# Two attentions on one core: an earlier place for ScalarE's copy in double steps, and B's output products in single steps

## The chip, the cores and the metric

The kernel runs on one core of one Trainium2 chip. The metric is the device time of one execution in microseconds. Before the change it was 1608.44 us, the median of 3 runs (1606.99 to 1608.65). The phase that the change touches runs from about 420 us to 1600 us of the profiled execution.

## What is computed

Two independent attention blocks over 2048 positions of width 576, with 32 heads of 18 columns each, side by side in the output:

```python
def _A_ref(x, wqkv, wo):            # window of 8 positions, 2 apart
    qkv = (x @ wqkv).reshape(B, S, 3, H, Dh)...
    logits = einsum("bhsd,bhswd->bhsw", q, kg) * scale      # kg, vg: 8 gathered positions
    attn = softmax(where(mask, logits, -1e9))
    return einsum("bhsw,bhswd->bhsd", attn, vg)... @ wo

def _B_ref(x, wqkv, wo):            # every position sees every position
    p = softmax(einsum("bhqd,bhkd->bhqk", q, k) * scale)
    return einsum("bhqk,bhkd->bhqd", p, v)... @ wo

return concatenate([a, b], axis=-1)
```

All inputs are fp32. The kernel splits fp32 operands of its matmuls into a rounded upper part and a remainder, and makes each product as three matmuls (upper by upper, upper by rest, rest by upper).

## The kernel before

**Three phases.** First the projections of both attentions (TensorE, until about 420 us). Then 512 steps in which B is computed and A runs beside it, mostly on GpSimd. Then a short close.

**A step.** B's work is ordered by head group (8 groups of 4 heads, `g`), block of 512 queries (4 blocks, `b`) and tile of 128 keys (16 tiles, `kt`). For one step TensorE makes four score matmuls, one per head (L269, into a bank of the ring "scores"), ScalarE makes four exponentials of them (L277, into tiles `e`), and TensorE makes the weighted sums of the step before it (`weigh`, L742): four matmuls side by side, one per head, on 32 columns each, into one bank `po` that collects the 16 steps of a block. A score works on 56 of 64 rows of the array; two of them, on the upper and the lower 64 rows, run side by side.

**The maxima.** The exponentials need a bound of each query's scores ahead of time. For that the scores of later blocks are computed a second time, in pieces (L158), and VectorE reduces each piece (L166, one bank at a time). A step takes three pieces: one behind the first score, one split over two halves (`parts_of_maximum`), and one behind the last score. In TensorE's program these stand among the scores. When all pieces are done (`sum(given) == total`), the steps are "paired": the weighted sums of two steps follow each other.

**The banks.** Seven PSUM banks in two rings: four for "scores", three for "else" (pieces, products). The eighth is `po`. An instruction of TensorE that takes a bank waits until ScalarE or VectorE has read what was there.

**Output products.** A product of 128 positions by 288 output columns with `wo` takes two strands of some 14 (A) or 15 (B) matmuls, one on the upper and one on the lower 64 rows. There are three ways in which they stand in the order:
- In a *double step* (`together`, L1174 to 1214): two steps are written as one. First the upper strand beside the scores of heads 1 and 3 of both steps, then the lower strand beside those of heads 0 and 2, each with a piece of the maxima per score. Both strands add into one bank, so a ScalarE nop with two semaphores stands between them. Then come the weighted sums of two steps at once. ScalarE's eight exponentials are written as soon as the next score is (`in_turn` keeps one pending), and behind them the copy of the finished product (L1212).
- *In a single step* (`beside`, L1054, called from `sum_of`, L1076, with a `kind`): both strands side by side into two banks, with two more pieces of the maxima between them, in front of the step's last score. VectorE copies one bank out and adds the other (L1090, L1093).
- *Loose* (`waiting`, without a `kind`): the same without the pieces; ScalarE copies the one bank (L1092), VectorE adds the other.

Which of them is used is decided by the loop at L1219 and the lines below it: if something stands in the list `inside`, at least 8 pieces are left and the step is not the first of its block, the step and the next become a double step (L1224); else a product in `inside` goes into a single step (L1249). A's products come from `finished` (L967), B's from `full` (L1121). There are 34 double steps, 32 with a product of A and two with one of B.

**A block's finished sums.** With the 16th step of a block `weigh` calls `finish` (L747), which has `po` copied into the tile `o`, so that the next block can use the bank. If a double step comes next, the copy is put into the list `leaving` (L752), and `together` places it among the exponentials (L1206): `upper` lists the scores and pieces of heads 0 and 2 in turn, and with `upper[4]` come the next score, the exponential that is pending, and the copy. That happens in 22 of the 34 double steps. One step later SP loads the denominators out of `o` (L781).

Of the kernel before, what the change touches and what calls it, by code (L numbers as in the profile page):

```python
# [33 lines left out]
ALL = NG * STEPS  # L34
# [25 lines left out]
def two_attentions(ctx: ExitStack, tc, xa, wa, woa, xb, wb, wob, out):  # L60
# [19 lines left out]
    def bank(kind=None):  # L80
        r = rings[kind or ring]
        r.append(r.pop(0))
        return p_bank.tile([128, 512], F32, name=f"bank{r[-1]}")
# [22 lines left out]
    step = 0  # L106

    def later(n, f):
        agenda[step + n].append(f)
# [104 lines left out]
    given = [0, 0]  # L214
# [93 lines left out]
    def halves(r, odd, w, x, wcols, xcols, weights_move=False):  # L308

        at = slice(64 * r, 64 * r + 64)  # L310
        both = [p for c in range(4) for p in pairs(c, w, x, wcols, xcols)] + pairs(4, w, x, wcols, xcols)[: 1 + (r == odd)]
        return [(b[at], a[at]) if weights_move else (a[at], b[at]) for a, b in both]
# [68 lines left out]
    with (tc.tile_pool(name="x", bufs=1, side="right") as xp,  # L381
# [103 lines left out]
        if True:  # L485
# [9 lines left out]
            chunks = [[(0, 0, 128)], [(0, 128, third - 128), (D, 0, 256 - third)], [(D, 256 - third, 128)]]  # L495
# [185 lines left out]
            for k in range(2, 14):  # L681
                n = 46 if k == 2 else 36 + 4 * k
# [7 lines left out]
            def leave_a(c, b, n, ps):  # L690
                o = xp.tile([128, 512], F32, name="ohi", bufs=4)
                nc.scalar.activation(o[:n], ps, AF.Copy)  # L692
                load(da[128 * c : 128 * c + n, HALO + 512 * b : HALO + 512 * b + 512], o[:n])
# [23 lines left out]
            for c, b in order:  # L717
                n = min(128, 3 * D - 128 * c)
                work_list.append(((b % 2, ws[c][0], xas[b][0], slice(0, n), every),
                                  lambda ps, n=n: ps[:n], lambda ps, c=c, b=b, n=n: leave_a(c, b, n, ps)))  # L720
# [12 lines left out]
        step = 0  # L733
# [130 lines left out]
    def local(j):  # L864
# [100 lines left out]
            x.append(last)  # L965

        def finished(h, n):  # L967
            inside.append(lambda alone: sums_of_a(h, n, alone))

        def sums_of_a(h, n, alone):  # L970
            his, los = zip(*wo["a"])
            w = his[:4], los[:4], his[4], los[4]
            cols = slice(288 * h, 288 * h + 288)
            if h == 0:
                st["y"] = ys["a", j, n] = work.tile([128, D], F32, name="y", bufs=4)
            y = st["y"][:, cols]
            both = [halves(r, 0, w, st["x", n], cols, slice(0, 128), True) for r in range(2)]
            if not alone:
                return both, y
            one, two = beside("scores", *both)  # L980
            nc.scalar.activation(y, two, AF.Copy)
            behind_scores.append(lambda: nc.vector.tensor_add(y, one, y))
# [25 lines left out]
    olds = defaultdict(list)  # L1008
# [25 lines left out]
    ys = {}  # L1034
# [12 lines left out]

    leaving = []

    inside = []  # L1050

    waiting = []
# [20 lines left out]
            rings["else"].append(rings["else"].pop(0))  # L1073
        return sums_

    def sum_of(y, t, h, chunks, kind=None, alone=True):  # L1076

        pos, cols = slice(128 * t, 128 * t + 128), slice(288 * h, 288 * h + 288)
        both = []
        for r in range(2):  # L1080
            both.append([])
            for c, (hi, lo) in enumerate(chunks):
                at = slice(64 * r, min(64 * r + 64, hi.shape[0]))
                whi, wlo = wo["b"][c]
                both[r] += [(a[at, pos], w[at, cols]) for a, w in ((hi, whi), (hi, wlo), (lo, whi))]
        if not alone:
            return both, y
        one, two = beside(kind, *both)
        if kind:
            nc.vector.tensor_copy(y, one)  # L1090
        else:
            nc.scalar.activation(y, one, AF.Copy)  # L1092
        nc.vector.tensor_add(y, two, y)  # L1093
# [27 lines left out]
    def full(b, new):  # L1121
        def half(t, h):
            if total - sum(given) > 4:
                inside.append(lambda alone: quarter(t, h, "scores", alone))
            else:
                waiting.append(lambda: quarter(t, h))

        def quarter(t, h, *kind):
            if h == 0:
                ys[t, b] = work.tile([128, D], F32, name="y", bufs=4)  # L1130
            if h == 1:
                later(1, lambda: load(out[512 * b + 128 * t : 512 * b + 128 * t + 128, D:], ys[t, b]))
            return sum_of(ys[t, b][:, 288 * h : 288 * h + 288], t, h, [*olds[b], new], *kind)

        return [(4 + 2 * t + h, lambda t=t, h=h: half(t, h)) for t in range(4) for h in range(2)]

# [31 lines left out]
    ready = [(0, 0, 0, es)]  # L1168
# [3 lines left out]
    total = early + rest  # L1172

    def together(both, y):  # L1174

        at = [(*divmod(s // NT, NB), s % NT) for s in (step, step + 1)]
        es = [[None] * 4 for _ in range(2)]
        ps = bank("scores")[:, : y.shape[1]]
        held = rings["scores"].pop()
        exps = deque()  # L1180

        def one(i, h):
            f = score(*at[i], h, put_off=True)
            exps.append(lambda: es[i].__setitem__(h, f()))

        def others(r):
            return [f for i in range(2) for h in (r, r + 2)
                    for f in (lambda i=i, h=h: one(i, h), lambda: maximum(r)())[:: 1 - 2 * r]]

        def piece(r, k):  # L1190
            a, b = both[r][k]
            return nc.tensor.matmul(ps, a, b, start=r == k == 0, stop=r == 1 and k == len(both[1]) - 1)  # L1192

        def in_turn(*lanes):

            for _, f in sorted(((at + every * k, f) for fs, at, every in lanes for k, f in enumerate(fs)), key=lambda p: p[0]):
                f()
                while len(exps) > 1:
                    exps.popleft()()

        last = []
        in_turn(([lambda k=k: last.append(piece(0, k)) for k in range(len(both[0]))], 0, 133), (others(1), 1, 235))
        between = nc.scalar.nop()
        sync(between, last[-1])
        upper = others(0)
        if leaving:  # L1206
            upper[4] = lambda f=upper[4], copy=leaving.pop(): (f(), exps.popleft()(), copy())
        in_turn(([lambda k=k: sync(piece(1, k), between) if k == 0 else piece(1, k) for k in range(len(both[1]))], 240, 133),
                (upper, 0, 235))
        while exps:  # L1210
            exps.popleft()()
        nc.scalar.activation(y, ps, AF.Copy)  # L1212
        rings["scores"].append(held)
        return [(*at[i], es[i]) for i in range(2)]
# [4 lines left out]
    while step < ALL:  # L1219
        n, kt = divmod(step, NT)  # L1220
        g, b = divmod(n, NB)
        es = [None] * 4

        if inside and kt and len(ready) == 1 and total - sum(given) >= 8 and step + 4 < ALL:  # L1224
            new = together(*inside.pop(0)(False))
            assert not leaving
            due()
            step += 1
            weigh(*ready, new[0])
            ready[:] = new[1:]  # L1230
            due()
            step += 1
            continue

        while leaving:
            leaving.pop()()

        whole = total - sum(given) > 1
        parts = (bool(begun) or total - sum(given) > 3) and step not in copied

        ps = bank() if inside and whole else None


        ahead = kt == 0 and (n < 6 or n >= 24)
        part = [parts_of_maximum()] if parts and not ahead else []
        for h in (0, 2, 1, 3):

            if inside and h == 3:
                inside.pop(0)(True)  # L1249
            es[h] = score(g, b, kt, h, between=(lambda: part.append(parts_of_maximum())) if parts and ahead and h == 0 else None)  # L1250
            if h == 0 and whole:
                maximum(1, ps)()
            if h == 1 and parts:
                part[0]()
            if h == 3 and whole:
                maximum(0)()
        if sum(given) == total and not begun:
            settle()
        for fs in (behind_scores, outside):
            while fs:  # L1260
                fs.pop(0)()

        paired = paired or kt % 2 == 0 and sum(given) == total and not begun
        for _ in range(1 if paired and step < ALL - 2 else len(waiting)):
            if waiting:
                waiting.pop(0)()
        if ready and (kt % 2 == 0 or not paired):
            weigh(ready.pop(0))
        ready.append((g, b, kt, es))
        if paired and kt % 2:  # L1270
            weigh(*ready)
            ready.clear()
        due()

        if len(waiting) > (0 if not paired else 2 if kt % 2 else len(waiting)):
            waiting.pop(0)()
        step += 1
# [24 lines left out]
```

## Time and profile before

| | |
|---|---|
| median of 3 runs | 1608.44 us |
| the profiled execution's own time | 1606.85 us |
| its span, first to last instruction | 1605.0 us |
| TensorE (PE) | 1587.4 us busy, 13320 matmuls |
| VectorE (DVE) | 1361.3 us busy, 2311 instructions |
| ScalarE (ACT) | 1215.2 us busy, 2440 instructions |
| GpSimd (POOL) | 959.8 us busy, 792 instructions |
| mean granted TensorE clock | 0.999 |

The profile is one execution. Its rows name the line of the kernel, the engine, the operation and output <- input. PE is TensorE's matmuls, PEld its weight loads. PE's busy time counts overlapped matmuls once, and their ends are modelled, so distances between starts say more than lengths. Idle time in brackets is that of the engine just before the instruction, with the instruction that ended it. In the trace a fp32 weighted sum is two instructions, so x8 at L742 is one step and x16 are two.

### The profile page before, as it was taken

How to read it: one execution, taken by the hardware profiler on the slowest of the kernel's cores; microseconds unless marked ns; L12 is line 12 of the kernel's file. 1: busy time of each engine (PE TensorE's matmuls, PEld its weight loads, DVE VectorE, ACT ScalarE, POOL GpSimd, SP SyncE). 2: the span in 40 equal slices, each digit the busy share in tenths (PEclk: the TensorE clock that was granted, in tenths of full speed). 3: DMA queues.
4: the chain of work that ended last, by engine and by line, in shares of the span. 5: the costliest groups of instructions: out<-in, count | busy, mean ns of one | idle time of the engine just before them, and what ended most of it. 6: DMA issues, size and time to landing. Idle time of an engine off the chain costs nothing.

```text
span 1605.0 us, 34995 instructions
## 1 busy us (share of the span) xinstructions
PE 1587.4 (99%) x13320; PEld 969.4 (60%) x13320; DVE 1361.3 (85%) x2311; ACT 1215.2 (76%) x2440; POOL 959.8 (60%) x792
## 2 busy tenths in 40 slices
PE   9999999999999999999999999999999999999998
PEld 7999889999543444444444445445445445445776
DVE  5199999999999999999899998999998999898422
ACT  6423441121699999999999999999999999998555
POOL 2405742210266995995896896897797797772100
PEclk9999999999999999999999999999999999999999
DMA  9937954532221362254326325422632231154111
GB/s 252 237 124 193 268 168 134 146 105 80 60 52 52 81 154 67 53 126 95 73 78 144 73 92 116 103 84 49 140 102 66 61 97 31 44 174 146 67 38 60
DMA packets 186056, 172.09 MB, mean 107 GB/s; under 512 B 119152, under 2 KB 132976, under 8 KB 184160
## 3 DMA queue, kind: packets, MB, share of 16 engines
q1 hardware_dynamic: 181024, 158.31, 36.0%
q0 software_dynamic: 4032, 10.63, 3.2%
q8 instruction: 104, 1.70, 0.5%
q10 hardware_dynamic: 832, 0.92, 0.2%
q14 instruction: 64, 0.52, 0.1%
HBM read 96.94 MB, written 71.90 MB: 105 GB/s over the span
## 4 chain that ended last, share of the span: by engine, by line
PE 86%; ACT 6%; DVE 4%; DMA 2%; issue 1%; POOL 1%; SPq 0%; POOLq 0%; DVEq 0%; ACTq 0%
PE po L742 29%; PE bank L269 17%; PE bank L158 16%; PE bank L364 15%; ACT e L277 5%; PE bank L301 5%; PE bank L1068 4%; DVE mx L166 3%; PE bank L1192 2%; ACT o L752 1%; POOL xlo L412 1%; DMA den<-o 0%; DMA dqk<-ohi 0%; DMA dqk<-olo 0%; DMA first<-xb 0%
## 5 line engine op out<-in xcount | busy, mean ns | idle before, releaser
L166 DVE TENSOR_REDUCE mx<-bank 128x2 f32<-128x512 f32 x2048 | 1278.8, 684 | 132.7 <-PE bank L158 99.4
L277 ACT ACTIVATE e<-bank 128x512 f32<-128x512 f32 x2048 | 1046.8, 607 | 69.5 <-PE bank L269 61.2
L158 PE MATMUL bank<-ks,qs 54*128 54x512 f32 (+1 forms) x2462 | 790.7, 382 | 4.4 <-DVE mx L166 3.2
L158 PEld LDWEIGHTS bank<-ks,qs 54*128 54x128 f32 x2462 | 403.5, 184 | 383.9 <-DVE mx L166 337.9
L269 PE MATMUL bank<-qs,ks 56*128 56x512 f32 x2048 | 597.7, 426 | 0.0
L742 PE MATMUL po<-e,v 128*19 128x512 f32 x4096 | 531.1, 598 | 3.2 <-ACT o L752 1.6
L269 PEld LDWEIGHTS bank<-qs,ks 56*128 56x128 f32 x2048 | 309.2, 184 | 32.2 <-ACT e L277 24.3
L887 POOL TENSOR_TENSOR pr<-aq,akv 128x1024 f32<-128x1024 f32 x72 | 158.3, 2200 | 15.7 <-DMA akv<-da 12.9
L742 PEld LDWEIGHTS po<-e,v 128*19 128x19 f32 x4096 | 73.9, 97 | 143.0 <-issue 129.5
L930 POOL TENSOR_TENSOR pr<-lg,akv 128x1024 f32<-128x1024 f32 x72 | 158.3, 2199 | 0.6
L891 POOL TENSOR_TENSOR pr<-pr 128x1024 f32<-128x1024 f32 x64 | 152.4, 2382 | 5.0
L692 ACT ACTIVATE ohi<-bank 128x512 f32<-128x512 f32 (+1 forms) x56 | 30.4, 595 | 150.9 <-issue 107.2
L364 PE MATMUL bank<-xhi,ahi 64*128 64x512 f32 (+1 forms) x448 | 114.9, 387 | 0.0
L364 PE MATMUL bank<-xhi,alo 64*128 64x512 f32 (+1 forms) x448 | 111.3, 387 | 0.0
L364 PE MATMUL bank<-xlo,ahi 64*128 64x512 f32 (+1 forms) x448 | 108.8, 388 | 0.1
L1192 PE MATMUL bank<-wohi,at 64*128 64x288 f32 x480 | 103.4, 305 | 0.0
L931 POOL TENSOR_TENSOR pr<-pr 128x512 f32<-128x512 f32 x72 | 92.4, 1283 | 5.6
L1192 PEld LDWEIGHTS bank<-wohi,at 64*128 64x128 f32 x480 | 74.7, 184 | 27.4 <-ACT e L277 23.8
L412 POOL TENSOR_TENSOR alo<-raw,ahi 128x512 fp32r<-128x512 f32 (+1 forms) x14 | 17.6, 1255 | 121.3 <-ACT ahi L411 86.5
L504 POOL TENSOR_TENSOR olo<-olo,ohi 128x512 fp32r<-128x512 f32 x36 | 46.1, 1293 | 63.8 <-ACT ohi L503 55.9
L1192 PE MATMUL bank<-wolo,at 64*128 64x288 f32 x240 | 70.1, 292 | 0.0
L101 POOL CAST mh<-mt 128x32 fp32r<-128x32 f32 x32 | 6.8, 213 | 102.4 <-DVE mt L183 102.4
(211 smaller groups left out, 1872.5 us busy)
## 6 DMA issues: line engine op xcount, KB each, us to landing
do<-n SPq DMA_DIRECT2D x28, 512.0 KB
da<-ohi SPq DMA_DIRECT2D x52, 256.0 KB
akv<-da SPq DMA_DIRECT2D x64, 175.5 KB
out<-y SPq DMA_DIRECT2D x32, 288.0 KB
qs<-dqk SPq DMA_DIRECT2D x30, 288.0 KB
ks<-dqk SPq DMA_DIRECT2D x30, 288.0 KB
at<-dao SPq DMA_DIRECT2D x60, 128.0 KB
rec<-drec SPq DMA_DIRECT2D x29, 256.0 KB
```

Source lines behind the costliest of these rows:

```text
L158: return nc.tensor.matmul(ps if part is None else ps[:, 256 * r : 256 * r + 256], qs[at, b, p, 128 * t : 128 * t + 128], ks[at, p, 512 * k ...
L166: nc.vector.tensor_reduce(at, ps.rearrange("q (s n) -> q s n", s=2), axis=AX.X, op=ALU.max)
L269: nc.tensor.matmul(ps, ks[at, p, 128 * kt : 128 * kt + 128], qs[at, b, p], start=True, stop=True)
L277: nc.scalar.activation(e, ps, AF.Exp, scale=SCALE)
L301: nc.tensor.matmul(ps, a, b, start=c == i == 0, stop=c == 4 and i == 1)
L364: nc.tensor.matmul(ps, a, b, start=start, stop=stop)
L742: nc.tensor.matmul(po[32 * i : 32 * i + 19], vs[g][:, kt, 19 * i : 19 * i + 19], es[i], start=kt == 0, stop=kt == NT - 1)
L887: nc.gpsimd.tensor_mul(pr, ap(st["q"][:, 2 * c], (SUB, 2), (0, W), (1, SUB)), window(st["k"], c))
L891: nc.gpsimd.tensor_add(st["pr"], st["pr"], pr)
L930: nc.gpsimd.tensor_mul(at, ap(st["lg"], (0, 2), (SUB, W), (1, SUB)), window(st["v"], c))
L931: nc.gpsimd.tensor_add(at[:, :, :4], at[:, :, :4], at[:, :, 4:])
L1192: return nc.tensor.matmul(ps, a, b, start=r == k == 0, stop=r == 1 and k == len(both[1]) - 1)
```

## The change

Two edits in the program's order; no matmul is added or taken away.

1. In `together` the copy of a block's finished sums goes from `upper[4]` to `upper[2]`: behind the double step's fifth exponential and no longer behind the sixth.
2. Only products of A may make a double step. A set `for_two` holds them, and the loop asks for it. B's products then always go into single steps or are loose, and `sum_of` loses the way that gave its strands to a double step.

```diff
         def finished(h, n):
-            inside.append(lambda alone: sums_of_a(h, n, alone))
-
-        def sums_of_a(h, n, alone):
+            inside.append(lambda *alone: sums_of_a(h, n, *alone))
+            for_two.add(inside[-1])
+
+        def sums_of_a(h, n, alone=True):
...
+    for_two = set()
+
...
-    def sum_of(y, t, h, chunks, kind=None, alone=True):
+    def sum_of(y, t, h, chunks, kind=None):
...
-        if not alone:
-            return both, y
         one, two = beside(kind, *both)
...
             if total - sum(given) > 4:
-                inside.append(lambda alone: quarter(t, h, "scores", alone))
+                inside.append(lambda: quarter(t, h, "scores"))
...
-            return sum_of(ys[t, b][:, 288 * h : 288 * h + 288], t, h, [*olds[b], new], *kind)
+            sum_of(ys[t, b][:, 288 * h : 288 * h + 288], t, h, [*olds[b], new], *kind)
...
         if leaving:
-            upper[4] = lambda f=upper[4], copy=leaving.pop(): (f(), exps.popleft()(), copy())
+            upper[2] = lambda f=upper[2], copy=leaving.pop(): (f(), exps.popleft()(), copy())
...
-        if inside and kt and len(ready) == 1 and total - sum(given) >= 8 and step + 4 < ALL:
+        if inside and inside[0] in for_two and kt and len(ready) == 1 and total - sum(given) >= 8 and step + 4 < ALL:
             new = together(*inside.pop(0)(False))
...
             if inside and h == 3:
-                inside.pop(0)(True)
+                inside.pop(0)()
```

## The prediction

> **What bounds the kernel now.** I read the page first (busy shares, the chain that ended last), then the list of waits, then the order in time around one double step with a copy and one without, and at last TensorE alone from 1485 us to 1530 us.
>
> ```profile
> PE 1587.4 (99%) x13320; PEld 969.4 (60%) x13320; DVE 1361.3 (85%) x2311; ACT 1215.2 (76%) x2440; POOL 959.8 (60%) x792
> ...
> PE 86%; ACT 6%; DVE 4%; DMA 2%; issue 1%; POOL 1%; SPq 0%; POOLq 0%; DVEq 0%; ACTq 0%
> PE po L742 29%; PE bank L269 17%; PE bank L158 16%; PE bank L364 15%; ACT e L277 5%; PE bank L301 5%; PE bank L1068 4%; DVE mx L166 3%; PE bank L1192 2%; ACT o L752 1%; POOL xlo L412 1%; DMA den<-o 0%; DMA dqk<-ohi 0%; DMA dqk<-olo 0%; DMA first<-xb 0%
> ```
>
> TensorE is busy 99% of the span and is 86% of the chain that ended last; the largest line of that chain is L742, the weighted sums (`weigh`). So time is won only where TensorE gets through its own queue sooner. The list of waits names the reasons for which a queue stood (us in total, times, longest):
>
> ```profile
> PEld po L742 <- ACT o L752: 8.3, 22, 0.4
> ```
>
> TensorE came to the first weights of a new block and waited for ScalarE's copy L752 of the old block 22 times, 0.38 us each. There are 22 double steps that carry a copy. The first of them in time (start, length, engine, instruction, idle time before it and who ended it):
>
> ```profile
> 619.45 3.10 ACT L277 ACTIVATE e<-bank 128x512 f32<-128x512 f32 x6 [0.23 <-PE bank L269]
> ...
> 622.41 0.62 ACT L752 ACTIVATE o<-po 128x512 f32<-128x512 f32 x1
> ...
> 622.65 0.29 PE L1192 MATMUL bank<-wohi,ahl 64*128 64x288 f32 x1
> 622.89 1.12 ACT L277 ACTIVATE e<-bank 128x512 f32<-128x512 f32 x2
> ...
> 623.09 1.91 PE L742 MATMUL po<-e,v 128*19 128x512 f32 x16
> ...
> 624.93 0.38 PE L158 MATMUL bank<-ks,qs 54*128 54x256 f32 x1
> ...
> 625.52 6.68 ACT L277 ACTIVATE e<-bank 128x512 f32<-128x512 f32 x13 [1.21 <-PE bank L269]
> 625.58 1.89 DVE L166 TENSOR_REDUCE mx<-bank 128x2 f32<-128x512 f32 x3 [1.15 <-PE bank L158]
> ```
>
> ScalarE runs six exponentials from 619.45, the copy from 622.41 to 623.03, then two more exponentials. TensorE issued its last product matmul at 622.65 and its first weighted sum at 623.09, 0.06 us behind the end of the copy: the copy sets that start. Afterwards ScalarE stands for 1.21 us and VectorE for 1.15 us, both for TensorE: behind this double step only TensorE is late, and what it gains there is handed on to all three.
>
> How much of the 0.44 us from 622.65 to 623.09 can go? Double steps without a copy show it (the first two rows; the last two are the last one with a copy):
>
> ```profile
> 1470.63 0.29 PE L1192 MATMUL bank<-wohi,aq 64*128 64x288 f32 x1
> 1470.86 1.91 PE L742 MATMUL po<-e,v 128*19 128x512 f32 x16
> ...
> 1476.66 0.29 PE L1192 MATMUL bank<-wohi,aq 64*128 64x288 f32 x1
> 1477.11 1.48 PE L742 MATMUL po<-e,v 128*19 128x512 f32 x12 [0.16 <-ACT o L752]
> ```
>
> From the last product matmul to the first weighted sum it is 0.23 us without a copy (1470.63 to 1470.86) and 0.45 us with one (1476.66 to 1477.11). All 34 double steps fall into these two kinds: 0.22 or 0.23 us in the 12 without, 0.38 to 0.46 us, mean 0.436, in the 22 with a copy, the first and the last of which are shown.
>
> **Edit 1: the copy one exponential earlier.** In `together` the copy goes from `upper[4]` to `upper[2]`. ScalarE's order 1 to 6, copy, 7, 8 becomes 1 to 5, copy, 6, 7, 8 in all 22 places; TensorE's own order stays. Six exponentials start in 2.96 us (619.45 to 622.41), so one is 0.49 us, and the copy would end at 623.03 - 0.49 = 622.54. TensorE is ready at 622.65 + 0.22 = 622.87: the copy is 0.3 us early. What is late next is TensorE's own handoff. Gain: 22 x (0.436 - 0.22) = **4.7 us**.
>
> Queued behind the copy now is the sixth exponential. It starts 0.48 us later than it did (the copy's place in the queue, 622.41 to 622.89) and ends near 623.0. TensorE needs it for the second of its two groups of weighted sums, which starts half of 1.84 us (623.09 to 624.93) behind the first, near 622.87 + 0.92 = 623.8. So the first group hides it, with 0.8 us to spare; what it costs without that cover is the third rival. Exponentials seven and eight and the product's copy start when they did. The copy itself waits for nothing late: `po` was last written a step before, and `o` is one of two buffers. No DMA and no instruction of SP or GpSimd changes its place here. I take no cost.
>
> The Trainium skill, "TensorEngine Tiling (Array Packing)", Key Properties, says that a change of the tiling mode drains TensorE. Products use 64 rows and weighted sums 32 columns, so by this rule the 0.22 us stay, as the rows say. The rule also speaks against edit 2, which adds such a change.
>
> **Edit 2: B's output products outside of double steps.** Nothing else changes before step 487 of 512. There two double steps (487/488 and 489/490) each held one product of B. In the changed order steps 487, 488 and 489 are single steps, each with a product and two more maxima beside it (L1249, `beside`); then follow a loose product, step 490 without one, and from 491 the paired tail, two steps sooner than before. By the start of step 494 eight products were done before and seven are after; the missing one comes in step 503. No matmul is added or removed, so what differs is stalls and handoffs. TensorE today, with two rows of VectorE:
>
> ```profile
> 1485.54 0.38 PE L158 MATMUL bank<-ks,qs 54*128 54x256 f32 x1
> 1486.23 0.39 PE L269 MATMUL bank<-qs,ks 56*128 56x512 f32 x1
> 1486.35 1.85 DVE L166 TENSOR_REDUCE mx<-bank 128x2 f32<-128x512 f32 x3
> 1486.57 1.05 PE L742 MATMUL po<-e,v 128*19 128x512 f32 x8
> 1487.56 0.40 PE L1192 MATMUL bank<-qs,ks 64*128 64x288 f32 x1
> ...
> 1500.95 0.29 PE L1068 MATMUL bank<-qs,ks 64*128 64x288 f32 x2
> 1502.96 0.39 PE L269 MATMUL bank<-qs,ks 56*128 56x512 f32 x1
> 1503.14 0.46 DVE L1090 COPY y<-bank 128x288 f32<-128x288 f32 x1 [1.50 <-PE bank L1068]
> 1504.22 0.40 PE L1068 MATMUL bank<-qs,ks 62*128 62x288 f32 x1 [0.74 <-DVE y L1093]
> 1506.86 0.39 PE L1068 MATMUL bank<-qs,ks 62*128 62x288 f32 x1 [0.37 <-ACT y L1092]
> ...
> 1519.66 0.40 PE L1068 MATMUL bank<-qs,ks 64*128 64x288 f32 x2
> 1521.76 0.63 PE L269 MATMUL bank<-qs,ks 56*128 56x512 f32 x4
> 1522.23 0.59 PE L1068 MATMUL bank<-qs,pr 64*128 64x288 f32 x2
> 1526.87 1.91 PE L742 MATMUL po<-e,v 128*19 128x512 f32 x16
> 1528.71 0.41 PE L1068 MATMUL bank<-qs,qs 64*128 64x288 f32 x2
> ```
>
> Before, steps 487 to 493 last from 1487.56 to 1519.66 = **32.1 us**. In them are two stalls, 0.74 and 0.37 us (1504.22, 1506.86), where loose products follow each other and a bank of sums must first be emptied by VectorE or ScalarE. After, built from these rows:
> - A single step with a product: 0.69 us to its last score (1485.54 to 1486.23), the product 2.01 (1500.95 to 1502.96), two inserted maxima, and the last score with its maximum, each taken as 0.34 (1486.23 to 1486.57), weighted sums 0.99 (1486.57 to 1487.56): 4.37. Three: 13.1.
> - The loose product: 2.1 (1519.66 to 1521.76). Step 490: 2.02 (1485.54 to 1487.56) and 0.37 for its bank, as at 1506.86: 2.4.
> - In the tail two paired steps with three products take 9.05 (1519.66 to 1528.71), and four scores 0.47 (1521.76 to 1522.23). Steps 492 and 493 with two products: 9.05 - 2.1 = 6.95. Step 491, four scores, one product and the sums of two steps: 9.05 - 2 x 2.1 - 0.47 = 4.4.
> - The product still owed: 2.1.
>
> Sum 13.1 + 2.1 + 2.4 + 4.4 + 6.95 + 2.1 = 31.05, a gain of **1.05 us**. This is an estimate, since no row of before shows a step of just this make. On the good side: no wait of its own in step 490, and inserted maxima that hide in the product, 0.37 + 3 x 0.34 = 1.4 more, and half as much again for what I overlook: a gain of 3 us. On the bad side: each of the three products stalls by 0.74 + 0.37, as today's loose ones do, 3.3 us, a loss of 2.3. I take the sum, whose rows have the very shapes. VectorE has the room: three maxima take 1.85 us, 0.62 each, and emptying a product takes two instructions of 0.46 (1503.14), so five maxima and these are 4.0 us in a step of 4.37. That is nearly full, but not the bound.
>
> Moved past each other on other queues: on SP one store of a row block of `out` (L1132) comes behind the eight loads of the last block's maxima (L195). Those maxima end one step sooner than before (490, not 491), and nobody reads `out`. I take nothing for either.
>
> One more group of weighted sums stands in steps 486 to 491 (five, before four). Two groups of one step are 2 x 0.99 = 1.98 against 1.84 for one of two steps, and a handoff is 0.22: 0.36 us, which is in the sum already. By the drain rule of the Trainium skill's page named above this 0.36 us is owed; if changes of mode were free, edit 2 would gain 1.4 us.
>
> **Sum.** 4.7 + 1.05 = 5.75 us. The profiled execution took 1606.85 us, 1.85 more than its span of 1605.0; it would take 1601.1. It lies 1.6 below the median of the runs shown, 1608.44; that less 5.75 is **1602.7 us**, faster by 0.36%.
>
> **Rivals.**
> - *The gain is given back.* Single steps keep ScalarE without a pause (13 exponentials in 6.68 us from 625.52), so a double step that ends sooner may only make TensorE wait for ScalarE. Against it: ScalarE itself stood 1.21 us for TensorE right behind the double step. Then only edit 2 counts: 1607.4 us.
> - *B's single products stall on banks.* For it: the stalls at 1504.22 and 1506.86, and VectorE's 4.0 of 4.37 us. Then edit 2 loses 2.3: 1608.44 - 4.7 + 2.3 = 1606.0 us.
> - *Slower: the sixth exponential becomes the one waited for*, in front of the second group of weighted sums in the 22 double steps. It decides once that exponential ends more than 0.8 us later than worked out above. A full price is the copy's 0.48 us less the 0.22 won, 0.26 us, 22 times = 5.7 us of loss: 1608.44 + 5.7 - 1.05 = 1613.1 us. Against it: the margin, and that ScalarE ran all six without a pause, so the scores are there in time.
> - *The change doesn't do what it says*: the 0.22 us are not the copy's. The 12 double steps without one speak against it. Its time is that of the first rival, and it shares its chance.
>
> **Numbers.** About 0.2% (3.2 us) is what a measurement of this kernel can tell from no change: faster is below 1605.2, slower above 1611.7. The forecast gets 0.70, the gain given back 0.12, the bank stalls 0.12, slower 0.06. So faster 0.70, same 0.24, slower 0.06. The range starts at 1608.44 - 4.7 - 3 = 1600.7, less 0.7 for the spread of the runs shown, 1600.0, and reaches over both middle rivals to 1607.6; only the slower one is left out.
>
> **What would show it.** Right: L742's wait for L752 is gone from the list; last product matmul and first weighted sum stand 0.22 us apart in all double steps; no new wait of L742 for an exponential L277; steps 487 to 493 take some 29 us with one product owed. Wrong: L742 waiting for L277; TensorE idle for VectorE in steps 487 to 489; or the 22 gaps closed and the start of step 487 still not 4 to 5 us earlier.

## The result, and the profile after

| | median | runs | ratio to before, 95% interval |
|---|---|---|---|
| before, same chip | 1608.65 us | 7 (1605.96 to 1610.69) | |
| changed | 1603.11 us | 7 (1601.25 to 1603.97) | 0.9966 [0.9954, 0.9977] |
| before, second measurement | 1608.71 us | 12 (1607.09 to 1611.22) | |
| changed, second measurement | 1603.90 us | 8 (1601.26 to 1605.94) | 0.9968 [0.9958, 0.9979] |

The change wins 5.5 and 4.8 us; 5.75 were predicted, to 1602.7 us. The profiled execution after took 1601.25 us (span 1599.4, granted clock 0.999 as before). In the changed kernel the products of double steps are at L1193 (they were at L1192), those of `beside` at L1071 (L1068), the copy of a double step's product at L1213, and the instructions that empty the banks of `beside` at L1091 and L1094 (VectorE) and L1093 (ScalarE). First the page: busy time, the chain that ended last by engine, and by line.

```profile
PE 1586.0 (99%) x13324; PEld 964.6 (60%) x13324; DVE 1363.5 (85%) x2315; ACT 1214.4 (76%) x2438; POOL 959.8 (60%) x792
...
PE 90%; DVE 4%; DMA 2%; ACT 2%; POOL 1%; issue 1%; SPq 0%; POOLq 0%; DVEq 0%
PE po L742 28%; PE bank L269 18%; PE bank L158 17%; PE bank L364 14%; PE bank L301 5%; PE bank L1071 4%; PE bank L1193 4%; DVE mx L166 3%; DMA den<-o 1%; ACT e L277 1%; POOL xlo L412 1%; DMA raw<-xa 0%; DMA dqk<-olo 0%; PE bank L516 0%; SPq L509 0%
```

ScalarE's share of the chain fell from 6% to 2%: L752, the copy, is gone from it, and the exponentials L277 fell from 5% to 1%. TensorE holds 90% of it now. One small entry has grown, from 0% to 1%, and will matter below: `DMA den<-o`, the load of the denominators. What L742's weight loads waited for, the two largest lines of it in the list of waits (us in total, times, longest):

```profile
PEld po L742 <- issue: 132.6, 536, 0.3
...
PEld po L742 <- DVE o L757: 2.0, 8, 0.3
```

The line `ACT o L752: 8.3, 22, 0.4` is gone, and the 22 handoffs have joined those for which nothing but TensorE's own issue is named (516 before, 538 with edit 1 alone, 536 with both). The first double step with a copy, in order of time (start, length, engine, instruction, idle time before it):

```profile
618.18 2.60 ACT L277 ACTIVATE e<-bank 128x512 f32<-128x512 f32 x5 [0.23 <-PE bank L269]
...
620.67 0.60 ACT L752 ACTIVATE o<-po 128x512 f32<-128x512 f32 x1
...
621.14 1.60 ACT L277 ACTIVATE e<-bank 128x512 f32<-128x512 f32 x3
...
621.39 0.29 PE L1193 MATMUL bank<-wohi,ahl 64*128 64x288 f32 x1
621.61 0.14 PEld L742 LDWEIGHTS po<-e,v 128*19 128x19 f32 x8 [0.17 <-issue]
621.61 1.91 PE L742 MATMUL po<-e,v 128*19 128x512 f32 x16
```

ScalarE runs five exponentials, the copy, three more. The copy ends at 621.27, 0.34 us before the weighted sums start; from the last product matmul to them it is 0.22 us (621.39 to 621.61), as in a double step without a copy. All 22 places show 0.21 to 0.23 us, mean 0.219. Now TensorE's rows at the borders of steps 487 to 493:

```profile
1482.93 0.38 PE L158 MATMUL bank<-ks,qs 54*128 54x256 f32 x1
...
1487.31 0.38 PE L158 MATMUL bank<-ks,qs 54*128 54x256 f32 x1
...
1491.61 0.38 PE L158 MATMUL bank<-ks,qs 54*128 54x256 f32 x1
...
1495.91 0.41 PE L1071 MATMUL bank<-qs,ks 64*128 64x288 f32 x2
...
1498.01 0.28 PE L158 MATMUL bank<-ks,qs 54*128 54x256 f32 x1
1498.66 0.50 PE L158 MATMUL bank<-ks,qs 54*128 54x512 f32 x1 [0.27 <-ACT y L1093]
...
1500.56 0.85 PE L269 MATMUL bank<-qs,ks 56*128 56x512 f32 x4
...
1505.18 0.73 PE L269 MATMUL bank<-qs,ks 56*128 56x512 f32 x4
...
1512.23 0.40 PE L1071 MATMUL bank<-qs,pr 64*128 64x288 f32 x2
```

Step 487 starts at 1482.93 and not at 1487.56. Steps 487 to 489 are single steps with a product each, 4.38, 4.30 and 4.30 us, without a gap for VectorE; then a loose product and step 490 with one wait of 0.27 us; step 493 ends at 1512.23.

**Where the time came from.** Three marks divide an execution: the first weighted sum (L742; the start of B's loop), the start of step 487, and the end. The kernels under the changed one in this table are described below. Times in us from the start of the span.

| kernel | first L742 | step 487 | span | first L742 to 487 | 487 to the end |
|---|---|---|---|---|---|
| before | 420.1 | 1487.56 | 1605.0 | 1067.5 | 117.4 |
| changed | 419.0 | 1482.93 | 1599.4 | 1063.9 | 116.5 |
| changed, again | 421.3 | 1486.93 | 1603.6 | 1065.6 | 116.7 |
| copy_only | 420.9 | 1484.27 | 1601.8 | 1063.4 | 117.5 |
| single_only | 420.2 | 1487.44 | 1604.3 | 1067.2 | 116.9 |
| copy_seventh | 421.1 | 1498.47 | 1616.0 | 1077.4 | 117.5 |
| copy_fourth | 420.4 | 1493.10 | 1609.7 | 1072.7 | 116.6 |
| two_idle | 423.4 | 1488.96 | 1605.5 | 1065.6 | 116.5 |
| four_idle | 424.0 | 1505.69 | 1622.5 | 1081.7 | 116.8 |
| no_flush | 421.4 | 1489.23 | 1606.2 | 1067.8 | 117.0 |
| den_later | 423.0 | 1485.35 | 1602.0 | 1062.4 | 116.6 |
| den_again | 420.1 | 1482.65 | 1599.3 | 1062.5 | 116.6 |

The first stretch has the same work in all of them up to one idle constant, and it scatters between 419.0 and 424.0 us. So of the 5.6 us between the two first profiles 1.1 lie in code that neither edit touches, so they count as scatter; 3.5 lie between the first weighted sum and step 487, where edit 1 works, and 1.0 behind it, where edit 2 does.

### The profile page after: what moved, and what is told of

It reads as the page before. It is cut to its first block, busy times and chain, and to the rows that moved or that the text cites. A ratio compares the mean times of both kernels' runs of the same rounds, so it can differ in the third digit from the quotient of the medians.

```text
span 1599.4 us, 35014 instructions
## 1 busy us (share of the span) xinstructions
PE 1586.0 (99%) x13324; PEld 964.6 (60%) x13324; DVE 1363.5 (85%) x2315; ACT 1214.4 (76%) x2438; POOL 959.8 (60%) x792
## 4 chain that ended last, share of the span: by engine, by line
PE 90%; DVE 4%; DMA 2%; ACT 2%; POOL 1%; issue 1%; SPq 0%; POOLq 0%; DVEq 0%
PE po L742 28%; PE bank L269 18%; PE bank L158 17%; PE bank L364 14%; PE bank L301 5%; PE bank L1071 4%; PE bank L1193 4%; DVE mx L166 3%; DMA den<-o 1%; ACT e L277 1%; POOL xlo L412 1%; DMA raw<-xa 0%; DMA dqk<-olo 0%; PE bank L516 0%; SPq L509 0%
## 5 line engine op out<-in xcount | busy, mean ns | idle before, releaser
L166 DVE TENSOR_REDUCE mx<-bank 128x2 f32<-128x512 f32 x2048 | 1278.7, 683 | 124.5 <-PE bank L158 91.8
L277 ACT ACTIVATE e<-bank 128x512 f32<-128x512 f32 x2048 | 1046.9, 607 | 66.2 <-PE bank L269 60.3
L158 PE MATMUL bank<-ks,qs 54*128 54x512 f32 (+1 forms) x2466 | 791.3, 382 | 5.8 <-DVE mx L166 4.2
L158 PEld LDWEIGHTS bank<-ks,qs 54*128 54x128 f32 x2466 | 404.0, 184 | 389.1 <-DVE mx L166 340.8
L269 PE MATMUL bank<-qs,ks 56*128 56x512 f32 x2048 | 596.0, 426 | 0.0
L742 PE MATMUL po<-e,v 128*19 128x512 f32 x4096 | 531.5, 599 | 0.0
L269 PEld LDWEIGHTS bank<-qs,ks 56*128 56x128 f32 x2048 | 309.1, 185 | 30.9 <-ACT e L277 24.6
L742 PEld LDWEIGHTS po<-e,v 128*19 128x19 f32 x4096 | 73.9, 97 | 138.0 <-issue 132.6
L1193 PE MATMUL bank<-wohi,at 64*128 64x288 f32 x480 | 103.5, 305 | 0.0
L1193 PEld LDWEIGHTS bank<-wohi,at 64*128 64x128 f32 x480 | 74.8, 184 | 27.5 <-ACT e L277 23.8
L1193 PE MATMUL bank<-wolo,at 64*128 64x288 f32 x240 | 70.1, 292 | 0.0
L364 PEld LDWEIGHTS bank<-xhi,ahi 64*128 64x128 f32 (+1 forms) x448 | 64.5, 182 | 3.9
```

Source lines behind the costliest of these rows:

```text
L158: return nc.tensor.matmul(ps if part is None else ps[:, 256 * r : 256 * r + 256], qs[at, b, p, 128 * t : 128 * t + 128], ks[at, p, 512 * k ...
L166: nc.vector.tensor_reduce(at, ps.rearrange("q (s n) -> q s n", s=2), axis=AX.X, op=ALU.max)
L269: nc.tensor.matmul(ps, ks[at, p, 128 * kt : 128 * kt + 128], qs[at, b, p], start=True, stop=True)
L277: nc.scalar.activation(e, ps, AF.Exp, scale=SCALE)
L364: nc.tensor.matmul(ps, a, b, start=start, stop=stop)
L742: nc.tensor.matmul(po[32 * i : 32 * i + 19], vs[g][:, kt, 19 * i : 19 * i + 19], es[i], start=kt == 0, stop=kt == NT - 1)
```

## The experiments

The theory: edit 1 removes a wait for the copy at 22 places, 0.22 us each, and edit 2 removes stalls in steps 487 to 493. Rivals: the gain of edit 1 is something else than the copy's place; the copy ahead of the sixth exponential merely moves the wait; the gain of edit 2 is only the order of the loose products. The first four kernels ran on one chip beside 25 runs of before (median 1608.88 us), the next four on another beside 21 (1609.52 us).

**Each edit alone.** copy_only is before with this line alone; single_only is the changed kernel with `upper[4]` put back.

```diff
-            upper[4] = lambda f=upper[4], copy=leaving.pop(): (f(), exps.popleft()(), copy())
+            upper[2] = lambda f=upper[2], copy=leaving.pop(): (f(), exps.popleft()(), copy())
```

> Edit 1 alone: the copy behind the fifth exponential, B's two products still in double steps. My theory: 22 waits of 0.215 us go, 4.7 us gross; in the trace of the changed kernel some 1.3 us of that were lost again at three places where VectorE came late (a wait for the DMA of den, two operations of A that took longer), so 3.4 to 4.7 us faster, ratio 0.997 to 0.998. All 34 handoffs at 0.22 us. Rival, that the gain is given back in the single steps: ratio 1.000.

> Edit 2 alone: B's products in single steps, the copy still behind the sixth exponential. My theory: about 1 us faster (0.97 us between the traces from step 487 to the end), ratio 0.9994, and 22 waits of L742 for L752 stay in the list. Rival, that all of the time won is edit 2's and the start's: ratio 0.997.

copy_only: 1604.54 us (9 runs), ratio 0.9973 [0.9963, 0.9982]. single_only: 1608.41 us (11 runs), 0.9995 [0.9986, 1.0004]. So edit 1 alone wins 4.3 us, and edit 2 alone wins an amount that the times can't tell from nothing. The wait list of single_only still has the copy, with the same sum as before:

```profile
PEld po L742 <- ACT o L752: 8.3, 22, 0.4
```

In copy_only that line is missing and every handoff is 0.21 or 0.22 us. Compared start by start with before, its weighted sums come 0.17 to 0.25 us earlier at each of the 22 double steps with a copy, and fall back by 0.54 and 0.34 us at 745.5 and 888 us of before, which is taken up below.

**The copy one exponential later.** Before, with the copy behind the seventh exponential in 21 of the 22 places (the last keeps its place).

```diff
-            upper[4] = lambda f=upper[4], copy=leaving.pop(): (f(), exps.popleft()(), copy())
+            k = 6 if step < 481 else 4
+            upper[k] = lambda f=upper[k], copy=leaving.pop(): (f(), exps.popleft()(), copy())
```

> The kernel before with the copy one exponential later, behind the seventh, in 21 of the 22 double steps (the 22nd stays as it was). If the copy's place sets TensorE's start there, each of the 21 gaps grows by one place in ScalarE's queue, 0.48 to 0.49 us, from 0.44 to 0.92 us: 10 us slower, ratio 1.006. Rival, that the wait is covered anyway: ratio 1.000.

1617.78 us (5 runs), ratio 1.0058 [1.0045, 1.0071]: 8.9 us slower than before. Its list of waits:

```profile
PEld po L742 <- ACT o L752: 18.6, 22, 0.9
...
PE po L742 <- ACT o L752: 13.5, 22, 0.7
```

The wait of the weight loads grew from 8.3 to 18.6 us, 10.3 us for 21 places: 0.49 us for one place further back in ScalarE's queue, the very time that the prediction gave one exponential. The stretch from the first weighted sum to step 487 grew by 9.9 us.

**The copy one exponential earlier still.** The changed kernel with the copy behind the fourth exponential.

```diff
-            upper[2] = lambda f=upper[2], copy=leaving.pop(): (f(), exps.popleft()(), copy())
+            upper[0] = lambda f=upper[0], copy=leaving.pop(): (f(), exps.popleft()(), copy())
```

> The changed kernel with the copy one exponential earlier still, behind the fourth. If what is left of the gap, 0.22 us, is TensorE's own handoff, nothing more is won: as the changed kernel, ratio 0.9966, gaps 0.22 us. Rival, that the copy still sets the start: gaps below 0.22 us and up to 22 x 0.22 = 4.8 us more, ratio 0.9936. Fifth and sixth exponential start 0.48 us later than before; should that reach the first sums of the second group, L742 waits for L277.

1612.2 us (11 runs), ratio 1.0020 [1.0011, 1.0029]: 9.1 us above the changed kernel's 1603.11 us. Theory and rivals had all left this open: TensorE's handoff keeps its 0.22 us, and still a double step takes 0.45 us more than with the copy behind the fifth. Its first one with a copy, in time:

```profile
621.73 0.59 ACT L752 ACTIVATE o<-po 128x512 f32<-128x512 f32 x1
622.21 2.08 ACT L277 ACTIVATE e<-bank 128x512 f32<-128x512 f32 x4
...
622.38 0.29 PE L1193 MATMUL bank<-wolo,at 64*128 64x288 f32 x1
622.87 0.18 PEld L269 LDWEIGHTS bank<-qs,ks 56*128 56x128 f32 x1 [0.43 <-ACT e L277]
622.87 0.49 PE L269 MATMUL bank<-qs,ks 56*128 56x512 f32 x1 [0.20 <-ACT e L277]
622.87 0.53 PE L1193 MATMUL bank<-wohi,at 64*128 64x288 f32 x2
...
623.38 0.29 PE L1193 MATMUL bank<-wohi,ahl 64*128 64x288 f32 x1
623.60 0.14 PEld L742 LDWEIGHTS po<-e,v 128*19 128x19 f32 x8 [0.17 <-issue]
```

The last score of the double step (L269 at 622.87) waits for an exponential, with the product's matmuls queued behind it: 0.49 us pass between two product matmuls that are 0.13 us apart elsewhere (622.38 to 622.87). Four banks serve the scores and one of them collects the product, so the eighth score takes the bank that the fifth exponential reads. With the copy in front of it, that exponential starts at 622.21 and not a copy's place earlier. The wait list agrees: `bank L269` waited for L277 on the weight side 69 times, 33.9 us, and 47 times, 24.6 us, in the changed kernel; 22 times more, once per copy:

```profile
PEld bank L269 <- ACT e L277: 33.9, 69, 0.8
```

By the trace, against before a double step with a copy is 0.23 us slower with the copy behind the fourth exponential, 0.22 faster behind the fifth, and 0.49 slower behind the seventh (the sixth was its place before). Of the places tried one wins. The row at 623.38 serves for one more reading: here the copy is over at 622.32, 1.3 us ahead, and the handoff is 0.22 us all the same. So it is TensorE's own, and none of the orders of ScalarE tried here shortens it.

**How much room the sixth exponential has.** The changed kernel with two or four copies of an idle tile on ScalarE behind the copy (added work, without use for the result).

```diff
+    idle = const.tile([128, 240], F32, name="idle")
+    nc.vector.memset(idle, 0.0)
...
-            upper[2] = lambda f=upper[2], copy=leaving.pop(): (f(), exps.popleft()(), copy())
+            upper[2] = lambda f=upper[2], copy=leaving.pop(): (f(), exps.popleft()(), copy(), [nc.scalar.activation(idle, idle, AF.Copy) for _ in range(2)])
```

> The changed kernel with two copies of a 128x240 tile onto itself on ScalarE behind the copy, in front of the sixth exponential, in the 22 double steps. They do no work for the result; they only hold the sixth, seventh and eighth exponential up, by an estimated 0.3 us each. In the changed kernel's trace the sixth exponential ends at 621.76 and the second group of weighted sums starts near 622.5: a margin of 0.7 us, so two are covered: as the changed kernel, ratio 0.9966, no wait of L742 for L277. Rival (the sixth exponential is the one waited for): slower by up to 22 x 0.6 = 13 us, ratio 1.005.

> The same with four such copies, some 1.2 us. The margin of 0.7 us is used up and the second group of weighted sums waits for the sixth exponential some 0.5 us, 22 times: 11 us slower than the changed kernel, ratio 1.003 to 1.004, and waits of L742 for L277 in the list. If the margin is larger than worked out: ratio 0.9966.

two_idle: 1608.74 us (10 runs), ratio 0.9996 [0.9987, 1.0005]. four_idle: 1624.15 us (4 runs), 1.0097 [1.0081, 1.0112]. First two_idle, then four_idle:

```profile
625.31 0.60 ACT L752 ACTIVATE o<-po 128x512 f32<-128x512 f32 x1
625.79 0.85 ACT L1211 ACTIVATE idle<-idle 128x240 f32<-128x240 f32 x2
...
626.24 1.98 PE L742 MATMUL po<-e,v 128*19 128x512 f32 x16
626.55 1.55 ACT L277 ACTIVATE e<-bank 128x512 f32<-128x512 f32 x3
```

```profile
625.87 0.60 ACT L752 ACTIVATE o<-po 128x512 f32<-128x512 f32 x1
626.34 1.72 ACT L1211 ACTIVATE idle<-idle 128x240 f32<-128x240 f32 x4
...
626.79 2.85 PE L742 MATMUL po<-e,v 128*19 128x512 f32 x16
...
627.97 1.55 ACT L277 ACTIVATE e<-bank 128x512 f32<-128x512 f32 x3
628.60 0.12 PEld L742 LDWEIGHTS po<-e,v 128*19 128x19 f32 x4 [0.82 <-ACT e L277]
```

In the changed kernel the sixth exponential starts 0.47 us behind the copy (620.67 to 621.14). Two idle copies make that 1.24 us, 0.77 more, and the 16 weighted sums take 1.98 us where they took 1.91: 0.07 us are lost, and the room is used up. Four make it 2.10 us, 1.63 more; the weights of the second group stand for 0.82 us in front of the sixth exponential, and the weighted sums take 2.85 us, 0.94 more. Both put the room at 0.7 us (0.77 - 0.07; 1.63 - 0.94), where the prediction had 0.8. By the starts of the rows four idle copies lose 20.4 us over the 22 places; the stretch to step 487 grew by 17.8 us against the changed kernel's first profile, so some of it comes back between the places. four_idle was expected to be 11 us slower than the changed kernel and is 20 to 21 us slower, since an idle copy holds the queue for 0.4 us (1.63 / 4) and not the 0.3 us estimated.

two_idle's time missed what was expected of it: its median is 5.6 us above the changed kernel's. The 0.07 us per place don't explain that. Followed start by start, most of them are made good within the next steps, and its stretch to step 487 is 1.6 us longer than in the changed kernel's first profile but as long as in its second (1065.6 us each). Both of these profiles lose some 2 us more than the first at 1453 to 1459 us of before, where VectorE waited longer for a DMA in both (2.13 and 2.27 us for 1.67; that wait is taken up below). In two_idle's profile the first weighted sum starts at 423.4 us, in four_idle's at 424.0, later than in most; den_later, without the idle constant, shows 423.0, so scatter reaches nearly as far. What the rest of the 5.6 us is stays open.

**Is edit 2 only the order of loose products?** Before, with only the loose products changed: never two in a row.

```diff
-        for _ in range(1 if paired and step < ALL - 2 else len(waiting)):
+        for _ in range(1 if step < ALL - 2 else len(waiting)):
...
-        if len(waiting) > (0 if not paired else 2 if kt % 2 else len(waiting)):
+        if len(waiting) > (2 if kt % 2 else len(waiting)):
```

> The kernel before, with B's two products in double steps and the copy behind the sixth, but loose products are no longer emptied two at once in step 491: one per step. My theory is that edit 2 gains because loose products no longer follow each other, not because of the way the products stand: then this wins about what edit 2 does, 0.7 to 1.6 us, ratio 0.999 to 0.9995, and the stalls of 0.74 and 0.37 us in front of L1068 are gone. Rival, the single steps themselves are the faster form: ratio 1.000, and the time from step 487 to 494 less the owed products stays at 32 us.

1607.36 us (11 runs), ratio 0.9990 [0.9981, 0.9998]. Of the two stalls of before (0.74 and 0.37 us) one is left, since step 491's product and the loose one behind it still follow each other:

```profile
1505.90 0.40 PE L1068 MATMUL bank<-qs,ks 62*128 62x288 f32 x1 [0.74 <-DVE y L1093]
```

The stretch behind step 487 is 117.0 us, against 117.4, 117.5 and 117.5 in the three kernels without edit 2 and 116.5 to 116.9, mean 116.66, in the eight with it. So edit 2 wins 0.8 us (117.5 - 116.66), and the loose products alone, by their one profile, 0.5: more than half of it, it seems, not all. The stalls that go fit that: 0.74 + 0.37 - 0.27 = 0.84 us with edit 2, 0.37 without its single steps.

**What edit 1 gives back.** 22 x 0.217 = 4.8 us were gained at the places, yet the stretch to step 487 became only 3.5 us shorter in the first pair of profiles, and less than 2 us in the second profile of the changed kernel. Followed start by start, the changed kernel falls back by 0.37 us at 745.5, 0.65 at 886 to 888 and 0.29 at 1453 us of before, 1.3 us in all. In its second profile it falls back by 2.9 us, 2.4 of them at 1453 and in the double step right behind, whose late start no row here explains. The place at 886 to 888 is taken up in the last section. At the other two stands VectorE's reciprocal of the denominators (before at 743 and 1451, then changed at 741 and 1447):

```profile
742.80 0.25 DVE L782 RECIPROCAL den<-den 128x16 f32<-128x16 f32 x1
...
1451.08 0.25 DVE L782 RECIPROCAL den<-den 128x16 f32<-128x16 f32 x1 [1.36 <-DMA den<-o]
```

```profile
741.34 0.25 DVE L782 RECIPROCAL den<-den 128x16 f32<-128x16 f32 x1 [0.50 <-DMA den<-o]
...
1446.71 0.25 DVE L782 RECIPROCAL den<-den 128x16 f32<-128x16 f32 x1 [1.67 <-DMA den<-o]
```

VectorE reaches the instruction before its data has landed and stands, 0.50 us where it did not stand before and 1.67 us for 1.36, with the maxima queued behind it. At the first of them VectorE is ready 2.0 us sooner than before (741.34 - 0.50 = 740.84 for 742.80), but SP issues the load of the denominators only 1.0 us sooner (at 728.75 for 729.78): the data doesn't come forward by as much as its reader. den_later is the changed kernel with the reciprocal and the two transfers behind it one step later:

```diff
-                      (8, lambda: nc.vector.reciprocal(den, den)),
-                      (9, lambda: load(drec[g, b].rearrange("i (p n) -> (i p) n", n=16), den)),
-                      (13, lambda: load(rec, rows(drec[g, b], (512, 4), (0, 32), (1, 512)))),
+                      (9, lambda: nc.vector.reciprocal(den, den)),
+                      (10, lambda: load(drec[g, b].rearrange("i (p n) -> (i p) n", n=16), den)),
+                      (14, lambda: load(rec, rows(drec[g, b], (512, 4), (0, 32), (1, 512)))),
```

> The changed kernel with the reciprocal of the denominators (L782), its store and the load of its broadcast one step later each. Of the 22 steps of 0.215 us that the changed kernel wins, 0.36 us came back at 745 us and 0.28 us at 1453 us, where VectorE stood for the DMA of den. My theory: a step more (2 us) covers that DMA; those two set-backs go, 0.5 to 1 us faster than the changed kernel and, with the 1.36 us that the kernel before waits there itself, up to 2 us: ratio 0.9955 to 0.9965, no wait of L782 in the list. Rival: the set-backs have another cause (GpSimd, or A's operations on VectorE): ratio 0.9966 and the same steps lost.

1601.7 us (5 runs), ratio 0.9958 [0.9946, 0.9971], and a stretch to step 487 of 1062.4 us. Then both once more on one chip, beside 12 runs of before at 1608.71 us:

> The changed kernel once more, as the base for the next kernel on the same chip. Its median should be 5.5 us below that of before (ratio 0.9966), if the first measurement holds.

> The changed kernel with the reciprocal of the denominators and the two transfers behind it one step later, again. Theory A, that the changed kernel gives back some 1 us because VectorE comes to the denominators before they have landed: 1 to 1.5 us below the changed kernel of the same call, ratio to before 0.9958. Theory B, that the set-backs in the profile are the scatter of one execution: the same median as the changed kernel, within 0.3 us.

The changed kernel took 1603.90 us, the later reciprocal 1601.72 us (5 runs, 1601.09 to 1604.53), ratio 0.9961 [0.9948, 0.9973]. The wait of L782 in the changed kernel's second profile, in the list of waits:

```profile
DVE den L782 <- DMA den<-o: 2.7, 2, 2.3
```

In both profiles with the later reciprocal the line is missing. Their stretch is 1062.4 and 1062.5 us, 5.1 below the mean of 1067.5 of the three kernels with neither edit 1 nor this (before, single_only, no_flush); that is all of the 4.8 us of the 22 places, and a little more, as before itself stands 1.36 us at 1451; 1.2 us still come back at other places. So theory A holds by the traces for the two waits, and both medians lie lower than the changed kernel's, by 1.4 and 2.2 us (1 to 1.5 were expected). The intervals of the ratios overlap, so by times alone it isn't settled. The version is the best that was measured.

## Why the prediction was right, point by point

- **The time.** 5.75 us were predicted, 5.5 and 4.8 measured. That the first came so near is in part luck: in the profiles the two stretches that the edits work in account for 3.5 + 1.0 us, and 1.1 us of the difference between the spans lie ahead of both.
- **What bounds the kernel.** Right: 0.22 us off TensorE's path at 22 places shortened the whole by most of that sum, and 0.45 and 0.94 us put onto it (copy_fourth, four_idle) lengthened it by most of theirs.
- **Edit 1, 22 x (0.436 - 0.22) = 4.7 us.** Right at the places: 22 x (0.436 - 0.219) = 4.8. The copy is 0.34 us early, predicted 0.3. The sixth exponential has 0.7 us of room, predicted 0.8. What the sum left out is what comes back: 1.3 us in the first pair of profiles, of which 0.66 lie at the two waits for the denominators, and 2.9 in the second profile. The step that missed these waits is "No DMA and no instruction of SP or GpSimd changes its place here. I take no cost": places stay, but steps that end sooner bring VectorE sooner to data that DMAs deliver in their own time.
- **TensorE's own handoff of 0.22 us.** Right, in all 32 double steps that are left, and with the copy 1.3 us early as well. The rule in the Trainium skill, "TensorEngine Tiling (Array Packing)", Key Properties, that a change of tiling mode drains TensorE, is in agreement with that row; that a drain is what takes the 0.22 us, no run shows. Whether the 0.36 us of the added group of weighted sums is its doing, no run shows.
- **Edit 2, 1.05 us.** Right in sign, somewhat too large: 0.8. By terms (predicted, measured): three single steps 13.1 and 12.98; loose product with step 490 4.5 and 4.65; step 491 4.4 and 4.62; steps 492 and 493 6.95 and 7.05. The three terms behind the single steps were too short, by 0.47 us together, with the one named wait of 0.27 in them. "No matmul is added or removed" was not exact: four steps became single, a single step splits one of its pieces in two, and L158 has 2466 matmuls for 2462.
- **The gain is given back (0.12).** Not as put: TensorE did not come to wait for ScalarE. A quarter (1.3 of 4.8 us) was given back in the first pair of profiles and more than half (2.9) in the second profile, but in the main behind VectorE, by a DMA's data and by instructions that waited for GpSimd.
- **B's single products stall on banks (0.12).** Wrong: no gap in front of a product's row in steps 487 to 489, and 0.27 us once in step 490.
- **Slower, the sixth exponential (0.06).** Not in this kernel. Its point of decision was right, as four_idle showed when it was forced. But there was a second mechanism with the same sign, which the prediction did not name: one exponential further ahead and the copy holds back the bank of the eighth score. Had edit 1 gone to `upper[0]`, the same argument would have forecast the same 5.75 us of gain, where copy_fourth, which has edit 2 as well, lost 3.3 against before.
- **The change doesn't do what it says.** Wrong: copy_only and copy_seventh move the time by the copy's place alone, 0.22 us down and 0.49 us up per place.

## What to carry to other kernels

When an instruction is moved ahead in an engine's queue, price two things: what it now holds back, and for each of those instructions both what waits for its result and what waits for the buffer that it frees; here the sixth exponential had 0.7 us of room in its result, and the fifth none in its bank. A gain on the bounding engine can bring the consumer of a DMA forward by more than its data, so look for waits with little or no slack behind the change. Before an odd length is put down to scatter, look at what the other engines run at that moment. For effects under a microsecond, compare stretches between fixed marks over all kernels that share the edit, since eight stretches told 0.8 us where the times could not.

## What the runs showed of the hardware that was not expected

Before B's loop, code that is the same in before, changed, copy_only and den_later took 419.0 to 423.0 us. And two instructions of VectorE with the same shapes had other lengths in two profiles. Before, then changed, each with GpSimd's rows:

```profile
881.05 1.28 POOL L785 TENSOR_TENSOR o<-o,rec 128x512 f32<-128x512 f32 x1 [4.74 <-DMA rec<-drec]
...
882.39 0.61 POOL L786 CAST n<-o 128x512 fp32r<-128x512 f32 x1
882.77 0.38 DVE L905 TENSOR_TENSOR as<-as 128x128 f32<-128x128 f32 x1
...
883.51 1.28 POOL L787 TENSOR_TENSOR n<-o,n 128x512 fp32r<-128x512 f32 x1
...
885.15 0.21 DVE L905 TENSOR_TENSOR as<-as 128x64 f32<-128x64 f32 x1
```

```profile
879.66 1.28 POOL L785 TENSOR_TENSOR o<-o,rec 128x512 f32<-128x512 f32 x1 [5.93 <-ACT e L277]
...
880.19 0.91 DVE L905 TENSOR_TENSOR as<-as 128x128 f32<-128x128 f32 x1
...
882.06 1.29 POOL L787 TENSOR_TENSOR n<-o,n 128x512 fp32r<-128x512 f32 x1
...
882.81 0.61 DVE L905 TENSOR_TENSOR as<-as 128x64 f32<-128x64 f32 x1
```

0.91 for 0.38 us and 0.61 for 0.21 us: 0.9 us longer together, which is where the changed kernel fell back by 0.65 us at 886 to 888 us of before. In the changed kernel both start while GpSimd is within an instruction of its own (L785, 879.66 to 880.94; L787, 882.06 to 883.35) and end 0.15 and 0.08 us behind its end. Before, the first started near the end of a shorter one (L786, over at 883.00) and ended 0.15 us behind it, and the second started while GpSimd ran nothing.

The whole line L905 follows this, 576 instructions in the twelve profiles. The 533 that start while GpSimd runs nothing take 0.20 to 0.22 us (64 columns), 0.28 to 0.29 (128) or 0.41 to 0.43 (256). The 43 that start within one of GpSimd's take up to 0.92 us and end, by their width, 0.08, 0.14 to 0.18 or 0.28 us behind its end. So these instructions of VectorE wait until GpSimd is done. The maxima L166, which read one operand out of PSUM, don't: they take 0.62 to 0.70 us with GpSimd at work or without.

How the two engines meet differs from kernel to kernel: no_flush, which has neither edit, shows 0.63 and 0.58 us at the same place. So the 0.65 us are not shown to be an effect of the change.
